# The last inverse step in operands of 128 rows, the last convolution ahead of the last attention rows, and a new order

## The chip, the core and the metric

The kernel runs on one core of one Trainium2 chip. The core has five engines that run side by side and wait for each other by semaphores: PE (matrix products, with a loader of weights shown as PEld), DVE and ACT (elementwise work; ACT alone has exp, sin and ln), POOL, and SP, which here only issues DMAs. Results of PE land in PSUM and have to be evicted by DVE or ACT into SBUF. The metric is the device time of one execution in microseconds (us), the median of several runs. A profiled execution also gives a span, first instruction to last, and a trace.

## What is computed

`x = A_u` has 2048 times and 512 channels (bf16). Two mixers read the same `x`, and a gate joins them:

```python
x = A_u
g = _sigmoid((x * gate_w).sum(-1, keepdims=True))
a = _A_ref(x, ...)      # S4 convolution: K[d,l] = Re sum_n C B dt exp(dt A l); y = irfft(rfft(u) rfft(K)); y + u * Dskip
b = _B_ref(x, ...)      # linear attention, 32 heads of 16, feature map [softmax(xW), softmax(-xW)], then @ wo
return g * a + (1 - g) * b
```

In `_A_ref` each channel has its own kernel `K` of 2048 times, a sum over 128 complex poles; the convolution is causal and padded to 4096. In `_B_ref` keys and queries go through `w_phi` and two softmaxes of 16 features, `kv` and `z` are sums over all times, and `o = phi_q kv / (phi_q z + 1e-6)`.

## The kernel before, in words

The 512 channels are cut into 4 quarters `Q` of 128 and 16 units of 32. The 2048 times are 16 blocks `j` of 128 rows of the tile `xT[time, j, Q, channel]`, which at first holds `x` and at the end the output. 512 rows (4 values of `j`) make one block `b` of the queries.

- **Head** (`prepare`, `keys_and_spectrum`, `attention_keys`). Parameters are loaded, sine tables are made on ACT (`TB`, `TI`, `TJ` for the transforms, `Ctab`, `Dtab`, `Gtab` for the poles), `x` is transposed (`xps`, `xT`), the spectrum of `x` is computed (`psAu`, `XAu`, `psBu`, `XU`) and written to DRAM as `XUd` (`xuw`), and the keys run through `pk2`, `ek2`, `vp2`, `vb2`, `kn2`. `gps` and `zps` are the products of the gate.
- **Queries** (`block(b, late)` in `plan_queries`). Blocks 0 to 2 are computed in the middle of the convolution, and the part of their result that belongs to Q = 3 is put into `xT` (`bs3`); for Q < 3 it is added inside the inverse step (`pya`). Block 3, the last 512 rows, is "late": `pqL`, `eqL`, `zsL`, the normalisers through DRAM (`awL`, `arL`, `emL`), `opsL`, `oTL`, and then `bpsL` with all 512 columns at once, into which the already computed convolution of Q < 3 is added out of `g.Y`. `bsg` scales its columns 0 to 383 by the gate, `outL` stores them; columns 384 to 511 (`bs3`) go to `xT` for the inverse step of Q = 3.
- **Convolution** (`plan_conv`). For each unit `kgen` builds the kernel: `A1`, `A2` (L1053) and, where `FOURS` has a 0, `A3` (L1064) make a table `A`; `Rh` (L1071) and `Rl` (L1075) make `R`; `kps` (L176) multiplies them (128 products, or 64 where `A3` has summed), `KD` and `XA` are evictions, `psA` the first transform. `transform` then works on a group of units: `psB`, `XK`, the product with the spectrum of `x` (`t`, L1185), `psz` and its eviction `Zr`, a write to DRAM (`zw`, L1230), a read back in another layout (`zr`, L1239, into `ZT`), the last inverse step `psy` (L1295) with the table `TJ`, and `ou` (L1320), which scales by the gate into `xT`. Groups: two pairs of units each for Q = 0, 1, 2, then units 12 and 13 together (64 channels), 14 alone (32 channels), and 15 alone, which does not go through DRAM (`pszn`, `Zn`, `psyn`).
- **Last inverse step.** In `psy` the even and the odd half of the 32 slots of a block sit in partitions 0 to 63 and 64 to 127 of `ZT` (`th` = 0 or 1), so each product uses 64 rows and 32 columns of PE: 4 products per `j`.

**What sets the order.** All work is first listed as nodes with `P.add` (engine, dependencies, the buffers it takes and drops) and `P.dma`. `Plan.run` then emits the nodes in the order written in the string `ORDER` (two digits per node), with `SIDES` choosing ACT or DVE for a node that may run on either, `RINGS` choosing the PSUM pool and `FOURS` the form of `kps`. The strings were found by a planner outside the file. On the chip each engine runs its own instructions in that order and waits by semaphores; SP and ACT issue DMAs in their order too, so a DMA that waits holds up those behind it. There are 8 lanes for DMAs in flight (`ln`): a DMA also waits for the one that used its lane before. When ACT changes between `T` (sine) and `L` (exp, ln), it loads another table (L65).

Of the kernel before, what the change touches and what calls it, by code (L numbers as in the profile page):

```python
# [43 lines left out]
def build_index_cols(nc, pool):  # L44
# [4 lines left out]
    f = pool.tile([128, len(want)], F32, name="if")  # L49
# [6 lines left out]
    return t, f, {name: f[:, k:k + 1] for k, (name, _, _) in enumerate(want)}  # L56
# [14 lines left out]
class Plan:  # L71

    DIGITS = "0123456789abcdefghijklmnopqrstuvwxyzABCDEFGHIJKLMNOPQRSTUVWXYZ-_"
    ORDER = ("0J0K0f0g0h0L0O0N0R0S2x0c0d0e0i0j0k1c1e0M1b000102030405090a0b1I1x0u0v0w0Y1d1o1z0U1f0x0y0z0V0P0W1A0607081p1B1q1J1K1Y0l0m0n"
             "0-0Z180_0X112P1g1-2y2N1Z2Q2B130r0s0t0A0B0C1_2A2O2C1y1C0o0p0q10190D0E0F2J2K2R1h1F1D0Q1G16122L2M2T2S2F142H2U2G171S2I2D2E2V"
             "2X2W152Y4v4w1N1O1r1s1t1i1j1k4u4B4C1E4J2v2w0G0H0I1H4F4K4D4N1Q0T1a2Z4E2-2_1U1V1P301W4G4x4O1M1l1m1n4L4M591X27314H1u1v1w4R4I"
             "28214P32335a1T344V4S3520224Q2324361L4T4U55374W4X4Z56254Y393a384-51574_521R58263b3d4y3c503e535h2z2a3f5d545i293g5l3h5b2b5e"
             "3J3i5c2d5f5g5t3j5j3k5k5m2e3l3m3n3K3o3p5u5n5o5v3L5w2f3M2c2g3q3v3r5p5x3w2o2h5q3x2i3y3C3z3A3B5r5y3E3D3s3t3u3N3P3F3Q3G3H3I3O"
             "2q3R3S2k3T2j3V3X3Y3U3W3Z3-2l3_5s402m412p4342442r2s4546472n484a4f2t494h2u4b4g4m4o4i704c4d4e4p727r4n7t5z7q7s4j4k4l4q4r4s5A"
             "5B5C5D5E4t5I6_5F5G5H714z734A7674777968696a6b7c5J78757d7a7i7e7D7j6c7b7f5K7g7E7h9a6d6e7F7J9c6f5L7R7S7T7k6g7l7u6h6z7v7K7x7w"  # L80
             "7A7m5M5N7n8O6i6j6k7-7_806A5O7y7z8X6B7B8P7o8Y5P7p7C6l6m6n6p6q6r6o6C7G7H7I8K7U7V7W6t5Q8M6u8L8Q7L8U5R8V8N6s5S5T5U5V8ZaD8R6D"
             "5W5X5Y7MaE916E6F927N7P7O7Q6G5-5_606H9d8S6v9e9m9n5Z8T9f61818W6I828-8_996w62836x6J6K6L6M6N6O9ba-90639j6Pb06y93946Q6R6S6465"
             "896T8h9k8a8i6U6V8485669o6W8b9s9g678c9h7X7Y7Z6XaA8daC9t6Y6Z6-9i8p8qazaB9l9D9E9Fa_9597b18j969p9q8r988kaFaM9raJ8687889u8l8s"
             "8e8f8gaGaN9vaKcw9w9y8m8n8o8t9xbb9zcyaHaIcxaLbcb2aOaSaTb3czaPb49MaQb89N8D9A9B9C9Ocob9aRaUbhcs9UaV9Vbd8u8v8w8x8y8zb58A8B8C"
             "9P9Q8E9G9H9I8F9R9S9T9Wb6cAcBcCa0a1djdk8G8H9J9K9La2bsbtbub7cDa8a9cEcF8I9XcGcHcIaWba9Y8Jbie8a3aaaXe9dsaba4bvbwbxbedl9Z9-9_"
             "bfdpaYdqdtaZbgacbjcpcJcKcLcNcOcPbkcMblbncQadaeafdmamctdybodncqbmbBbCbJbKa5a6a7dobRbpbqbrbDdrcubEbSduagahaid7d8d9bFbLbMdz"
             "bZbNbybzbAanb-dvdwdxcrbTcvdAdBbUb_bGbHbIc0eaaobObPbQajakaldCbVeeefc1dEbWbXbYapdFdDdGebecaqc2c3c4ardOdHdPasdadbdceddIegeB"
             "eCeEeFdQdJdgdhdicbeDeheHeic5c6c7eGeIejdKcccddRcRekdSdddedfeJeKc8c9cacedLdMdNeLeMeNeOcfelemencScgcTdTdUdVchePeQeoawaxayeR"
             "cUeSatauaveTepdWdXdYcVcWdZd-d_cZcXcYclcmcneUeVc-e0eWeqeresc_d0cicjcke1d1d2d3eXeYeteuevewexeyeZe5e6e7e2e3e4e-e_d4d5d6ezeA"
             "f3f4f5f0f1f2")  # L90
    SIDES = ("101001110101011000000100111001111100000011000100010000111101010000000100001100000000010000000000000000000000100000000001"
             "00010111111100000001100101000000010")
    RINGS = ("001011011111010000001010010001001010010010100100100100000110001100010101011110011011000000000000000000001110000000000001"
             "01011110001100000000010111010011100111001011001010010100111100000111110")
    FOURS = ("0111111101111110")
# [96 lines left out]
def prepare(P, nc, g, evict, psum):  # L192
# [38 lines left out]
    S("ifc", lambda: nc.scalar.copy(out=F.fi[:], in_=F.ii[:]), r="ic0", w="ic1")  # L231
# [5 lines left out]
    def cols(e):  # L237
# [8 lines left out]
        e.tensor_scalar(out=o[:, 6:7], in0=b6, scalar1=-2.0 / 2048.0, scalar2=1.0 / 2048.0, op0=ALU.mult, op1=ALU.add)  # L246
        e.tensor_scalar(out=o[:, 8:12], in0=g.c128[:, 0:4], scalar1=g.icol["s5"], scalar2=None, op0=ALU.is_equal)
# [17 lines left out]
    def sine(out, v, kv, w, turn=False):  # L265
        S("tgs", lambda: act(out=out(), in_=(low(v()) if not turn else low(v()).rearrange("p (h t) -> p t h", h=2)), func=ACT.Sin, scale=TURN), r=kv, w=w, tab="T")
# [266 lines left out]
def keys_and_spectrum(P, nc, g, psum):  # L533
# [9 lines left out]
    for h in range(2):  # L543
# [30 lines left out]
        for r0 in range(0, 32, 4):  # L574
# [22 lines left out]
            def wr(h=h, r0=r0, box=box):  # L597
                for n, a in ((128, 0), (64, 128)):
                    nc.sync.dma_start(out=g.XUd[:, h, a:a + n, r0 - 4:r0 + 4, :].rearrange("d x r c -> x d (r c)"), in_=box.s[0:n].rearrange("p d r c -> p d (r c)"))
                box.s = None  # L600
# [30 lines left out]
def attention_keys(P, nc, g, psum, r):  # L631
# [19 lines left out]
    a = P.add("PE", "gps", ga, xt, take=[("ps", "b2")], rw=("wsm", ""))  # L651
# [125 lines left out]
def plan_queries(P, nc, g, psum, r):  # L777
# [14 lines left out]
    def block(b, late, yn=()):  # L792
# [110 lines left out]
        def out_mm(ps, i, j):  # L903
            for m in range(4):
                nc.tensor.matmul(ps, lhsT=g.oT[3][i // 2][:, m, 128 * (i % 2):128 * (i % 2) + 128], rhs=g.wo[:, m, :], start=(m == 0), stop=False,  # L905
                                 skip_group_check=True)
            nc.tensor.matmul(ps[:, 384:512], lhsT=xT[:, j, 3, :], rhs=at.diagD[:, 3, :], start=False, stop=True, skip_group_check=True)
            nc.tensor.matmul(ps[:, 0:384], lhsT=g.ident[:], rhs=g.Y[:, i].rearrange("p q d -> p (q d)"), start=False, stop=True, skip_group_check=True)
# [16 lines left out]
        for ip in range(2 if late else 0):  # L925
# [8 lines left out]
            def b3(j=j, box=box):  # L934
                return xT[:, j:j + 2, 3, :], box.ps[:, :, 384:512]

            def bg(k, j=j, box=box):
                o, i = xT[:, j + k, 0:3, :].rearrange("p k d -> p (k d)"), box.ps[:, k, 0:384]
# [12 lines left out]
        if late:  # L951
            def st(h):
                for c in (2 * h, 2 * h + 1):
                    (nc.scalar if P.cur.at == "ACT" else nc.sync).dma_start(out=g.out2d[:, 0:384].rearrange("(q j c) d -> c q j d", q=32, j=16, c=4)[c][:, 4 * b:4 * b + 4],
                                      in_=xT[32 * c:32 * c + 32, 4 * b:4 * b + 4, 0:3, :].rearrange("p j a d -> p j (a d)"))
# [64 lines left out]
def plan_conv(P, nc, g, psum, r):  # L1020
# [6 lines left out]
    T, on, yn, late = {}, [], [], []  # L1027

# [11 lines left out]
    def kgen(units, XA, new, split=False):  # L1040
# [58 lines left out]
        for cc in range(nu):  # L1099
# [24 lines left out]
            s = P.add("PE", "psA", sa, d + ([s] if cc else []) + ([XA.first] if XA.off else []), take=[psq] + (["XA0"] if new and cc == 0 and XA.off == 0 else []), drop=(["KD"] if cc == nu - 1 else []))  # L1124
# [5 lines left out]
    def load(Q, p):  # L1130
# [3 lines left out]
        def dma():  # L1134
            L.X = g.fpool.tile([128, 2, 1024], BF16, name="XUX", tag="XUX", bufs=g.P.k["XUX"])
            for i in range(2):
                if Q < 3:
                    nc.sync.dma_start(out=L.X[:, i].rearrange("p (h z) -> p h z", h=2), in_=g.XUd[Q, :, 64 * i:64 * i + 128, 8 * p:8 * p + 8, :].rearrange("h x r c -> x h (r c)"))
                else:
# [5 lines left out]
    def transform(XA, ready, Q, off, nd, far, Ls, last, co=0, free=True, split=False):  # L1145
# [122 lines left out]
        for j0 in range(0, 16, nj):  # L1268
# [75 lines left out]
            if two:  # L1344
                yn.append(P.add(("ACT", "DVE"), "Y", lambda oy=oy: P.copy(*oy()), [ya[0], y, o], drop=["psum"]))
# [227 lines left out]
```

## Time and profile before

| what | value |
|---|---|
| median of 3 runs | 270.79 us (268.94 to 270.85) |
| the profiled execution | 270.31 us, span 268.5 us |
| DVE busy | 224.2 us (83%), 300 instructions |
| ACT busy | 219.1 us (82%), 265 instructions, 23.1 us of them 18 table loads |
| PE busy | 202.2 us (75%), 4640 products; weight loads 140.5 us (52%) |
| DMA | 36.27 MB, mean 135 GB/s |

How to read it: the rows of groups give line, engine, operation, result <- operands with partitions x elements, the count, then busy us and mean ns of one, then idle time of the engine just before and what ended it. Rows of the timeline give start, length, engine, line, operation, and idle time before with its releaser in brackets. An x2 merges two neighbours. A row of the waits gives who waited for whom, the total in us, how often, the longest. "SPq" and "ACTq" are DMA issues; their length is the time of the issue, not of the transfer.

### The profile page before, as it was taken

How to read it: one execution, taken by the hardware profiler on the slowest of the kernel's cores; microseconds unless marked ns; L12 is line 12 of the kernel's file. 1: busy time of each engine (PE TensorE's matmuls, PEld its weight loads, DVE VectorE, ACT ScalarE, POOL GpSimd, SP SyncE). 2: the span in 40 equal slices, each digit the busy share in tenths (PEclk: the TensorE clock that was granted, in tenths of full speed). 3: DMA queues.
4: the chain of work that ended last, by engine and by line, in shares of the span. 5: the costliest groups of instructions: out<-in, count | busy, mean ns of one | idle time of the engine just before them, and what ended most of it. 6: DMA issues, size and time to landing. Idle time of an engine off the chain costs nothing. (4 is left out here: it accounts for less than half of the span.)

```text
span 268.5 us, 10262 instructions
## 1 busy us (share of the span) xinstructions
PE 202.2 (75%) x4640; PEld 140.5 (52%) x4640; DVE 224.2 (83%) x300; ACT 219.1 (82%) x265; POOL 7.6 (3%) x16
## 2 busy tenths in 40 slices
PE   1358999999886679758587877876978779789810
PEld 1247666566655434435466755464747547665600
DVE  6999768698999789999999989995999889976401
ACT  6899799989899899999999989996788897644100
POOL 7300000000000000000000000000000000000000
PEclk9999999999999959999569999996897999999955
DMA  5999510000439894048055441392686899998372
GB/s 116 145 179 224 143 42 2 1 2 2 120 95 257 243 277 160 5 115 213 6 166 147 105 156 35 128 173 68 196 258 188 168 219 246 201 235 151 60 110 44
DMA packets 71468, 36.27 MB, mean 135 GB/s; under 512 B 50304, under 2 KB 66304, under 8 KB 71424
## 3 DMA queue, kind: packets, MB, share of 16 engines
q1 hardware_dynamic: 67680, 34.83, 56.0%
q10 hardware_dynamic: 3744, 0.79, 1.6%
q8 instruction: 36, 0.59, 0.9%
q14 instruction: 8, 0.07, 0.1%
HBM read 21.12 MB, written 13.11 MB: 127 GB/s over the span
## 5 line engine op out<-in xcount | busy, mean ns | idle before, releaser
L1053 DVE TENSOR_TENSOR A<-Ctab,Dtab 128x2048 bf16<-128x2048 bf16 x32 | 38.3, 1221 | 0.2
L68 ACT ACTIVATE cs<-args 128x1024 bf16<-128x1024 f32 x32 | 30.9, 1037 | 1.9 <-issue 1.1
L65 ACT ACT_TABLE_LOAD x18 | 23.1, 1283 | 0.3
L176 PE MATMUL kps<-R,A 128*32 128x64 bf16 x1856 | 20.3, 202 | 3.3 <-issue 2.1
L176 PEld LDWEIGHTS <-A 128*32 128x32 bf16 x1856 | 18.3, 116 | 6.6 <-issue 5.3
L1071 DVE TENSOR_TENSOR R<-E,cs 128x2048 bf16<-128x2048 bf16 x16 | 19.5, 1220 | 0.6 <-ACT E L68 0.6
L140 ACT CAST XK<-psB 128x1024 bf16<-128x1024 f32 (+1 forms) x15 | 14.3, 980 | 6.5 <-PE psB L189 6.3
L1075 DVE TENSOR_TENSOR R<-El,cs 128x2048 bf16<-128x2048 bf16 x16 | 19.5, 1220 | 0.1
L1185 DVE TENSOR_TENSOR t<-XUX,XK 128x2048 bf16<-128x2048 bf16 x14 | 17.1, 1220 | 2.1 <-ACT XK L140 1.3
L1217 PE MATMUL psz<-t,TI 128*128 128x512 bf16 x60 | 16.1, 395 | 2.8 <-ACT cs L68 2.6
L806 PE MATMUL pq<-xT,Wqp 128*128 128x512 bf16 x64 | 15.8, 393 | 2.6 <-ACT KD L140 2.2
L140 ACT CAST Zr<-psz 128x1024 bf16<-128x1024 f32 x15 | 15.3, 1032 | 2.7 <-PE psz L1217 1.2
L140 ACT CAST XA<-psA 128x1024 bf16<-128x1024 f32 (+1 forms) x15 | 13.9, 972 | 3.9 <-PE psA L183 3.8
L189 PE MATMUL psB<-XA,TB 128*128 128x128 bf16 (+2 forms) x192 | 11.2, 207 | 7.3 <-issue 3.3
L68 ACT ACTIVATE Ek<-pk 128x1024 bf16<-128x1024 f32 x16 | 15.4, 1024 | 1.4 <-PE pk L679 1.3
L68 ACT ACTIVATE E<-args 128x1024 bf16<-128x1024 f32 x16 | 16.4, 1042 | 0.2 <-PE args L1004 0.2
L68 ACT ACTIVATE Eq<-pq 128x1024 bf16<-128x1024 f32 x16 | 15.5, 1061 | 0.6 <-PE pq L806 0.6
L1320 DVE TENSOR_TENSOR xT<-psy,gT 128x1024 bf16<-128x1024 f32 (+1 forms) x5 | 5.6, 1116 | 11.8 <-PE psy L1295 11.8
L710 PE MATMUL vp<-WW,xT 128*128 128x512 bf16 x64 | 15.0, 379 | 0.0
L679 PE MATMUL pk<-WW,xT 128*128 128x512 bf16 x64 | 15.0, 379 | 0.0
L189 PEld LDWEIGHTS <-TB 128*128 128x128 bf16 x192 | 9.4, 100 | 9.7 <-issue 9.2
L497 PE MATMUL xps<-ident,UD 128*128 128x128 bf16 x64 | 7.3, 293 | 7.6 <-DMA UD<-in_A_u_dram 5.6
(203 smaller groups left out, 488.6 us busy)
## 6 DMA issues: line engine op xcount, KB each, us to landing
XUX<-XUd SPq DMA_DIRECT2D x32, 256.0 KB, 4.3
XUd<-xst SPq DMA_DIRECT2D x8, 512.0 KB, 4.4
ax<-apd SPq DMA_DIRECT2D x16, 256.0 KB, 5.2
Zd<-Zr SPq DMA_DIRECT2D x15, 256.0 KB, 3.6
ZT<-Zd SPq DMA_DIRECT2D x6, 512.0 KB, 7.2
UD<-in_A_u_dram SPq DMA_DIRECT2D x16, 128.0 KB, 4.3
XUd<-xst SPq DMA_DIRECT2D x8, 256.0 KB, 5.4
out_dram<-xT SPq DMA_DIRECT2D x4, 192.0 KB, 4.2
```

What stands on the lines that cost most here:

```text
L65: return self.nc.scalar.preload_act_table_set(name)
L68: return self.nc.scalar.activation(**kw)
L140: self.nc.scalar.copy(out=o, in_=i)
L176: nc.tensor.matmul(kps[32 * dj:32 * dj + 32, g4, e, :], lhsT=A[:, d // 4, 32 * ka:32 * ka + 32, d % 4], rhs=R[:, kr, d, :], start=(i == 0) ...
L189: nc.tensor.matmul(ps[:, sl, :], lhsT=fc.TB[:, 3 * (r0 + sl) + 1:3 * (r0 + sl) + 3].rearrange("p a b -> p (a b)"), rhs=XA[:, r0 + sl], sta ...
L679: nc.tensor.matmul(box.ps[:, u, :], lhsT=xT[:, 2 * s2 + u, kt, :], rhs=g.WW[:, kt, :], start=(kt == 0), stop=(kt == 3))
L806: nc.tensor.matmul(box.ps[:, m - m0, :], lhsT=g.Wqp[:, kt, 128 * m:128 * m + 128], rhs=xT[:, 4 * b:4 * b + 4, kt, :], start=(kt == 0), sto ...
L1053: nc.vector.tensor_tensor(out=c.A[:, :, 64 * k:64 * k + 64, :].rearrange("p q (x b) l -> p x b q l", b=8), in0=cf.unsqueeze(2).to_broadcas ...
L1071: nc.vector.tensor_tensor(out=c.R[:, :, :, 32:64], in0=t.E[:].unsqueeze(1).to_broadcast([128, 2, 32, 32]), in1=t.cs[:], op=ALU.mult)
L1075: nc.vector.tensor_tensor(out=c.R[:, :, :, 0:32], in0=t.L[:].unsqueeze(1).to_broadcast([128, 2, 32, 32]), in1=t.cs[:, ::-1, :, ::-1], op=A ...
L1185: nc.vector.tensor_tensor(out=box.t, in0=Ls[r0 // ns].X[:], in1=box.XK[:].unsqueeze(1).to_broadcast([128, 2, 1024]), op=ALU.mult)
L1217: nc.tensor.matmul(box.ps[:, hb, :], lhsT=fc.TI[:, k].rearrange("p t h a -> p (t h a)"), rhs=box.t[:, k, 512 * hb:512 * hb + 512], start=( ...
```

## The change

1. **The last inverse step of the far groups** takes 128 rows: `ZT` now holds the (x, r) rows of one time pair in all 128 partitions, 16 slots per read, and `TJ` is masked once (`tjm`) so that odd slots keep only the upper, even slots only the lower 64 rows. Two products per `j` of 128 rows and 64 columns replace four of 64 x 32. Since unit 15 still needs the unmasked table, it is saved to DRAM first (`tjw`) and read back as `TJ2` into one of the 4 `cs` buffers (`tjr`). `TI` changes its inner order to suit.
2. **Units 12 to 14 go ahead of block 3.** For them `psy` takes blocks `j` < 12 from `xT` as before and for `j` = 12 to 15 only the skip term; the result for these four goes to `g.Y` (now 4 quarters), and `bpsL` adds it: 480 columns out of `g.Y`, 32 from the skip term. `bsg` scales 480 columns, `outL` stores 448, the last store (units 14 and 15) waits for `bsg` as well.
3. **Layouts.** `XUd` is laid out so that a load of Q < 3 is one DMA with runs of 2 KB. `ZT` of 64 channels takes an `XUX` buffer and of 32 channels a `Zr` buffer instead of the single `ax`.
4. **A new order**, new sides, rings and forms: `FOURS` sums the tables of units 0, 6, 12 and 14 instead of 0, 8 and 15.

```diff
-    FOURS = ("0111111101111110")
+    FOURS = ("0111110111110101")
...
-    a = P.add("PE", "gps", ga, xt, take=[("ps", "b2")], rw=("wsm", ""))
+    a = P.add("PE", "gps", ga, xt + [sp], take=[("ps", "b2")], rw=("wsm", ""))
...
-            nc.tensor.matmul(ps[:, 384:512], lhsT=xT[:, j, 3, :], rhs=at.diagD[:, 3, :], start=False, stop=True, skip_group_check=True)
-            nc.tensor.matmul(ps[:, 0:384], lhsT=g.ident[:], rhs=g.Y[:, i].rearrange("p q d -> p (q d)"), start=False, stop=True, skip_group_check=True)
+            nc.tensor.matmul(ps[:, 480:512], lhsT=xT[:, j, 3, :], rhs=at.diagD[:, 3, 96:128], start=False, stop=True, skip_group_check=True)
+            nc.tensor.matmul(ps[:, 0:480], lhsT=g.ident[:], rhs=g.Y[:, i].rearrange("p q d -> p (q d)")[:, 0:480], start=False, stop=True, skip_group_check=True)
...
+    def tjw():
+        g.TJd = g.dram.tile([128, 64, 32], BF16, name="TJd")
+        nc.sync.dma_start(out=g.TJd[:], in_=fc.TJ[:])
+
+    def tjm():
+        nc.vector.tensor_scalar(out=fc.TJ[:, 1::2, :], in0=fc.TJ[:, 1::2, :], scalar1=g.icol["b6"], scalar2=None, op0=ALU.mult)
+        nc.vector.tensor_scalar(out=fc.TJ[:, 0::2, :], in0=fc.TJ[:, 0::2, :], scalar1=g.icol["nb6"], scalar2=None, op0=ALU.mult)
...
+            if Q < 3:
+                d = g.XUd[Q, p]
+                nc.sync.dma_start(out=L.X[:], in_=bass.AP(d.tensor, d.offset, [[1024, 128], [64 * 1024, 2], [1, 1024]]))
+                return
...
+        zt = {128: "ax", 64: "XUX", 32: "Zr"}[nd]
...
-            nc.sync.dma_start(out=F.Z[64 * th:64 * th + 64], in_=F.Zd[:, 2 * th:2 * th + 2].rearrange("t x r d -> (x r) t d"))
+            nc.sync.dma_start(out=F.Z[:, 16 * th:16 * th + 16], in_=F.Zd[16 * th:16 * th + 16].rearrange("t x r d -> (x r) t d"))
...
                     for jj in range(nj):
-                        th = (j0 + jj) // 8
-                        rows = slice(64 * th, 64 * th + 64)
-                        for c in range(4):
-                            nc.tensor.matmul(box.py[32 * c:32 * c + 32, jj // nr, jj % nr, :], lhsT=fc.TJ[rows, 4 * (j0 + jj) + c, :],
-                                             rhs=F.Z[rows, 4 * (j0 - 8 * th + jj) + c, :], start=False, stop=True, tile_position=(64 * th, 32 * c),
-                                             skip_group_check=True)
+                        for c in range(2):
+                            m = 2 * (j0 + jj) + c
+                            nc.tensor.matmul(box.py[64 * c:64 * c + 64, jj // nr, jj % nr, :], lhsT=fc.TJ[:, 2 * m:2 * m + 2, :].rearrange("p h q -> p (h q)"),
+                                             rhs=F.Z[:, m, :], start=False, stop=True, tile_position=(0, 64 * c), skip_group_check=True)
...
-    late += r["block"](3, True, yn)
+
+    def tjr():
+        g.TJ2 = g.csp.tile([128, 64, 32], BF16, name="TJ2", tag="cs", bufs=4)
+        nc.sync.dma_start(out=g.TJ2[:], in_=g.TJd[:])
+    g.tjr = P.dma("tjr", 0.45, 2.0, tjr, [g.tjw, sq], take=["cs"], move=1.8)
     L, first = [load(3, p) for p in range(4)], None
     for k, (units, far) in enumerate(g.LAST):
...
+        if XA.drop:
+            late += r["block"](3, True, yn)
         done = kgen(units, XA, True, units in g.SPLIT)
```

Where the order puts the nodes that the prediction speaks of: on PE the end is now `kps` of unit 15, `psA`, `psz` of unit 14, `psB32`, `pya`, `psy128`, `pya` (both halves of Q = 2), the first half of `pszn`, `psy64`, `opsL`, `psy128`, `psy32` (unit 14), the second half of `pszn`, `bpsL` twice, `psyn32` twice. Before it was `kps` of unit 15, the second half of Q = 2, `psA`, `psy128`, `opsL`, `psB32`, `psz` of unit 14, `bpsL` twice, `pszn`, `psy64`, `psyn32` twice, `psy32`. On SP the reads of unit 14 follow its write with one other read between, and the stores of the output come behind them. In the head the table loads of ACT in front of the first `E` go from 8 to 13 (one more, at L231, is the same in both), behind it from 10 to 7.

More of the change, by code (lines that the diff above doesn't have):

```diff
@@ L1344, in transform @@
             if two:
[L1345 removed]
+                yn.append(P.add(("ACT", "DVE"), "Y", lambda oy=oy: P.copy(*oy()), (ya or [y]) + [y, o], drop=["psum"]))
+            if end and Q == 3 and last:
+                on.extend(r["on"])
             if end and Q != 0 and (nd > 32 or last):
```

113 lines of the change are left out of this document (61 added, 52 removed).

## The prediction

> **What bounds the kernel now.** I read the table of stages first: busy time of each engine in four stretches that I cut at two instructions of VectorE (DVE): the first table product of unit 0 (L1053, at 99.71) and the end of the last right-hand product of unit 15 (L1075). Columns: stretch, its length, busy PE, PEld, DVE, ACT, POOL, then the granted clock of PE, DMA share and GB/s.
>
> ```profile
> span 268.5 us, 10262 instructions
> 0.00:99.70 99.70, 77.07 (x1043) 52.51 (x1044) 85.02 (x151) 90.19 (x116) 7.59 (x16) 0.97 0.55 122
> 99.70:235.20 135.50, 106.62 (x2967) 74.74 (x2966) 126.19 (x131) 122.24 (x140) 0.00 (x0) 0.92 0.59 148
> 235.20:255.00 19.80, 16.99 (x559) 12.36 (x558) 11.83 (x17) 6.66 (x11) 0.00 (x0) 0.99 0.74 149
> 255.00:268.50 13.50, 1.56 (x74) 0.93 (x73) 1.12 (x2) 0.00 (x0) 0.00 (x0) 0.50 0.54 78
> ...
> 233.94 1.22 DVE L1075 TENSOR_TENSOR R<-El,cs 128x2048 bf16<-128x2048 bf16 x1
> ```
>
> Three regimes. In the head DVE is idle for 99.7 - 85.0 = 14.7 us and ACT for 9.5, both waiting on each other and on PE. In the middle DVE is the bound: 126.2 of 135.5, idle 9.3. From 235.2, where the last right-hand product ends (233.94 + 1.22; call that moment T), nothing is dense: 33.3 us in which DVE works 13. So the head and the middle are priced by work moved onto or off DVE and ACT, and the tail by its chain of waits. For that I read the instructions in order of time.
>
> ```profile
> 244.72 1.03 ACT L140 CAST Zr<-psz 128x1024 bf16<-128x1024 f32 x1
> 245.88 0.43 SPq L1230 DMA_DIRECT2D Zd<-Zr  x1
> 253.19 0.84 SPq L1334 DMA_DIRECT2D out_dram<-xT  x2
> 257.00 2.56 SPq L1239 DMA_DIRECT2D ZT<-Zd  x2
> 263.05 0.40 PE L1295 MATMUL psy<-ZT,TJ 64*32 64x32 bf16 x32 [1.64 <-DMA ZT<-Zd]
> 263.55 0.69 DVE L1320 TENSOR_TENSOR xT<-psy,gT 128x512 bf16<-128x512 f32 x1 [6.36 <-PE psy L1295]
> 264.27 1.27 ACTq L1334 DMA_DIRECT2D out_dram<-xT  x2
> ...
> SPq L1334 <- DMA out_dram<-xT: 7.1, 2, 6.9
> SPq L1239 <- DMA out_dram<-xT: 2.8, 1, 2.8
> ```
>
> Unit 14's last block is evicted at 244.72 and written at 245.88, but its read back (L1239) is issued only at 257.00: SP stands in front of output stores and of that read until earlier stores have landed (the last two rows, from the waits of the DMA queues). The read's second half reaches PE at 263.05, DVE scales at 263.55, the store follows. The end hangs on when that read is issued. Earlier in the tail PE ran block 3 of the attention (bps).
>
> **The change, part by part.**
>
> *The head (to 99.7).* The new order changes sides. By count of the nodes in front of unit 0's first product, DVE takes on two more XU evictions, two more vb2, one xT copy, selE and diagD (from POOL) and two maskings of TJ, and gives up one wpe. ACT gets the mirror image and five more table loads (13 for 8).
>
> ```profile
> L142 DVE CAST xst<-psB 128x1024 bf16<-128x1024 f32 x8 | 9.6, 1221 | 1.8 <-DMA XUd<-xst 1.4 <-PE psB L587 0.3
> L140 ACT CAST xst<-psB 128x1024 bf16<-128x1024 f32 x8 | 7.8, 1047 | 0.0
> DVE  6999768698999789999999989995999889976401
> L375 DVE TENSOR_TENSOR Dtab<-Dtab,trg 128x1024 bf16<-128x1024 bf16 x8 | 5.3, 686 | 0.1
> L413 DVE TENSOR_SCALAR Ctab<-Ctab 128x1024 bf16<-128x1024 bf16 x2 | 0.8, 423 | 0.0
> L65 ACT ACT_TABLE_LOAD x18 | 23.1, 1283 | 0.3
> 27.36 1.76 PE L641 MATMUL gps<-gw,xT 128*128 128x1 bf16 x64
> ```
>
> DVE: 4 - 1 = 3 casts of this size at 1.22 = 3.7; selE, diagD and xT at no more than the 0.69 of a bf16 1024 row = 2.1; two maskings at 0.42 = 0.8: +6.6. ACT: 5 x 1.28 = 6.4, less four casts at 1.05, the wpe and the xT cancelling: +2.2. The gate's product gps (1.76 on PE) no longer stands in front of the first key product, so the key stage starts up to 1.8 earlier, and its time comes back later in a stage in which PE waits anyway. If DVE's 14.7 and ACT's 9.5 us of idle time cover everything, the head gains 1.8; if DVE's additions all lie on the path, it loses 6.6. I take +1: ACT, the fuller engine, gets 2.2 more, less 1.8, rounded up, since DVE, in the row of busy tenths (40 slices of 6.7 us), reads 9 8 9 9 9 in the slices 9 to 13 and has little room late in the head.
>
> The rule against it: the Trainium skill, "ScalarE: Activation LUTs", section "What ACT_TABLE_LOAD costs", puts a switch of set at about 2.66 us, 1.28 for the load and 1.38 for a drain. The trace does not show the second half:
>
> ```profile
> 71.92 1.28 ACT L65 ACT_TABLE_LOAD   x1
> 73.22 2.01 ACT L68 ACTIVATE trg<-pb 128x1024 bf16<-128x1024 int16 x2
> ```
>
> The next activation starts 1.30 after the load. By the page the five loads would cost 13.3 and ACT would be 9.1 heavier, its whole idle time; the row decides, and the sum stays.
>
> TJ is also copied to DRAM before it is masked, one more DMA of 512 KB on SP among the stores of the spectrum, and read back later as TJ2. SP's own issue time is small there, but behind the copy stands the read of statE and behind that the next spectrum store; the spectrum's buffers number three. Priced at 0, bounds 0 and the 1.4 us that DVE waited for such a store (the xst row). The loads of the spectrum shrink from two DMAs to one of twice the run length; DVE waits 0.7 in all for them (the row below), so 0 to -0.7, taken 0.
>
> *The middle (99.7 to T).* Per node: DVE loses one KD, one XA and one XK cast, gains another KD cast, loses unit 15's sum of tables (L1064) and gains those of units 6, 12 and 14 for that of 8, so one more of 1.22 net; one scaling (ou of Q = 1) moves behind T.
>
> ```profile
> L1064 DVE TENSOR_TENSOR A<-A 128x2048 bf16<-128x2048 bf16 x3 | 3.7, 1221 | 0.0
> DVE t L1185 <- DMA XUX<-XUd: 0.7, 1, 0.7
> 187.08 1.23 DVE L1320 TENSOR_TENSOR xT<-psy,gT 128x1024 bf16<-128x1024 f32 x1 [2.84 <-PE psy L1295]
> ```
>
> (1 + 1 - 1 - 1 - 1 - 1) x 1.22 = -2.4 on the bound engine. ACT gets two casts more and four loads less up to there, and has 13.3 us of idle time. The price of the new order itself, the stalls that it brings or takes, no row shows. Below: the one large stall (2.84, ending at 187.08 with an inverse step) goes. Above: as many stalls again as now, +9.3. I take none either way.
>
> The inverse step proper: 32 products of a 64*32 tile become 16 of a 128*64 tile with half the weights zero. That shape stands in the trace as psA:
>
> ```profile
> 239.98 0.63 PE L1295 MATMUL psy<-ZT,TJ 64*32 64x128 bf16 x32
> 239.41 0.64 PE L183 MATMUL psA<-W,KD 128*64 128x128 bf16 x16
> ```
>
> 0.63 against 0.64: no time on PE, fewer instructions. That the read now fills 128 partitions instead of 64 twice may speed it; I take the old time.
>
> *The tail (from T).* Before: T to the end is 33.3. After, in the new order, the tables of unit 15 are unsummed (128 products), then KD, psA, unit 14's psz and its eviction and write follow at once, and SP stands in front of nothing but reads:
>
> ```profile
> 228.73 0.39 PE L787 MATMUL psy<-wo 128*128 128x128 bf16 x4
> 231.87 0.64 PE L183 MATMUL psA<-W,KD 128*64 128x128 bf16 x16
> 226.21 1.39 PE L176 MATMUL kps<-R,A 128*32 128x64 bf16 x128
> 238.60 0.37 ACT L140 CAST KD<-kps 128x256 bf16<-128x256 f32 x1 [2.64 <-DVE KD L142]
> 243.57 1.02 PE L1217 MATMUL psz<-t,TI 128*128 128x512 bf16 x4
> Zd<-Zr SPq DMA_DIRECT2D x15, 256.0 KB, 3.6
> 244.44 1.03 PE L905 MATMUL bps<-wo,oT 128*128 128x512 bf16 x4
> 248.85 2.31 PE L1251 MATMUL psz<-TI,t 128*32 128x64 bf16 x128
> L942 DVE TENSOR_SCALAR xT<-bps,gT 128x384 bf16<-128x384 f32 x4 | 2.3, 612 | 1.5 <-ACT xT L140 1.5
> 253.11 0.64 PE L1308 MATMUL psy<-Z,TJ 64*32 64x16 bf16 x64
> 251.28 0.88 ACTq L954 DMA_DIRECT2D out_dram<-xT  x2
> ```
>
> 1. kps 1.4 + two KD 0.7 + psA 0.6 + psz 1.0 + eviction 1.0 = T + 4.7 (before: 245.75 - 235.2 = T + 10.5, since oT, XK and half of bps' operands came between).
> 2. Write 3.6, then the two reads as now, from 257.00 to 263.05 = 6.05, then psy 0.4: T + 14.8.
> 3. What PE has meanwhile: the 17.0 of the third stretch, less bps (248.85 - 244.44 = 4.4), half of pszn 1.2 and psyn 2 x 0.64 = 1.3, plus the first half of Q = 2, today done before T (pya from 228.73 to 231.87 = 3.1, psy 0.6), plus 0.7 for the longer kps: at most 14.5. PE comes to this psy about when the read has landed; neither waits long.
> 4. Behind psy on PE: the other half of pszn 1.2, bps 4.4: T + 20.4. Its wait for the copied result of unit 14 (Y, on ACT) lies beside pszn and the first products.
> 5. ACT: one copy 0.4, two scalings of 480 instead of 384 columns at 0.7: T + 22.2. Then six DMA issues, 0.88 + 0.88 + 1.27 = 3.0, and from the end of the last issue to the end of the span what it is now, 268.5 - 265.54 = 3.0: T + 28.2. The branch over psyn, DVE and SP ends before that: psyn 1.3, a scaling and SP's own two issues.
>
> The tail gains 33.3 - 28.2 = 5.1. The wait that is added stands on PE: psy of unit 14 is ahead of pszn, bps and psyn, and everything behind it moves one to one with the read.
>
> **Sum.** The profiled execution took 270.31 (span 268.5 + 1.8 around it): + 1 - 2.4 - 5.1 = -6.5, so 263.8. The median shown, 270.79, is 0.5 above the profiled one; I forecast **264.3**.
>
> **The rivals.**
>
> *The head pays in full* (0.13). DVE's +6.6 all on the path: 270.8 + 6.6 - 2.4 - 5.1 = 269.9, no change. For it: the 9 8 9 9 9 above. Against: 14.7 us of idle time, and ACT, not DVE, is the fuller engine.
>
> *New stalls in the middle* (0.12). The order was laid out anew for 966 old and 9 new nodes; as many stalls again as today's 9.3 give 264.3 + 9.3 = 273.6, at the border of slower. For it: TJ2 holds one of the four cs buffers to the end and its read stands on SP ahead of the last write of Q = 0. Against: the engine loads are the same.
>
> *The last read is late and PE goes slow* (0.13), the case on the other side. Place: psy of unit 14, now ahead of bps. If SP queues as it does now, from the write at 245.88 to psy's end at 263.45, 17.6 us pass instead of 10.1: psy ends at T + 22.3 instead of 14.8. It decides from T + 20 on, where the gain of the tail is gone. And PE would then have stood for over 7 us: in the last stretch, where it waited so, the granted clock is 0.50 against 0.99 before it. pszn and bps (5.6) at half the clock cost 5.6 more: 264.3 + 7.5 + 5.6 = 277.4. The Trainium skill, "TensorE: Matmul & The Clock Gate", section "HAM oscillation", has the same rule, half clock after an idle window of some 3.4 us; by that rule even a wait of that length would do, and the row agrees. Against it: in the new order of SP, unit 14's two reads have no store of the output in front of them.
>
> *Better than that* (0.07): the stall at 184 goes too and the head gains its 1.8: 264.3 - 2.8 - 2.8 = 258.7. *The 128-row step does nothing by itself*: that is in the forecast already, at 0.
>
> **How the numbers follow.** Forecast case 0.55, better 0.07, head 0.13, middle 0.12, late read 0.13. Within 1%, about what a measurement of this kernel tells from no change, is 268.1 to 273.5. Faster: 0.55 + 0.07 = 0.62. No change: the head and 0.05 of the middle, 0.18. Slower: the rest of the middle and the late read, 0.20. Range 258 to 275: it takes in better, head and middle and leaves out the late read and a little below, under 0.2.
>
> **What the profile will show.** Right: unit 0's first table product at 99 to 102; the end of the last R<-El product at 232 to 236; SP's read of unit 14 issued within 5 us of its write; psy of 32 columns about 15 us after T; some 13 us from there to the end, bps in it at a clock near 1. Wrong: a first table product after 105 (head), DVE idle for over 15 us in the middle, SP waiting for stores in front of L1255 or a clock of 0.5 under bps.

## The result

The changed kernel takes 262.46 us (median of four executions, 261.1 to 266.1) against 270.8: 0.9691 of the time before, with a 95% interval of 0.9625 to 0.9758. It is **faster by 3.1%**, 1.8 us below the forecast of 264.3. The changed kernel's first profile fell on its longest execution, so the rows here are from its repeat (`again`, profiled at 261.36 us); the only other profile below that is of a kernel's longest execution is that of `pd3` (263.96 us).

### The profile after

First the stretches of the repeat, cut at the same two instructions as before and then within the tail (columns as in the prediction: after the busy times come the granted clock of PE, the DMA share and GB/s):

```profile
0.00:101.90 101.90, 77.56 (x1033) 54.17 (x1043) 89.52 (x162) 92.75 (x117) 3.99 (x13) 0.92 0.55 125
101.90:228.67 126.77, 100.53 (x2731) 68.66 (x2737) 123.30 (x129) 119.70 (x139) 0.00 (x0) 0.96 0.57 164
228.67:235.60 6.93, 4.10 (x187) 3.29 (x189) 3.04 (x4) 3.74 (x6) 0.00 (x0) 1.00 0.67 120
235.60:239.00 3.40, 3.40 (x36) 3.33 (x33) 1.89 (x3) 0.01 (x1) 0.00 (x0) 0.51 0.85 169
239.00:259.60 20.60, 14.04 (x425) 10.32 (x424) 8.55 (x15) 3.19 (x6) 0.00 (x0) 0.91 0.70 115
```

Head 101.9 (was 99.7), middle 126.8 (135.5), tail 259.6 - 228.67 = 30.9 (33.3). The gain stands in the middle, not in the tail where I had put most of it. In the middle VectorE's work fell by 126.19 - 123.30 = 2.9 and its idle time from 9.31 to 126.77 - 123.30 = 3.47, by 5.8.

The tail in order of time, same kernel:

```profile
227.44 1.23 DVE L1089 TENSOR_TENSOR R<-El,cs 128x2048 bf16<-128x2048 bf16 x1
...
233.42 0.61 PE L1233 MATMUL psz<-t,TI 128*128 128x512 bf16 x2 [1.88 <-DVE XA L144]
234.10 1.01 ACT L142 CAST Zr<-psz 128x1024 bf16<-128x1024 f32 x1 [2.26 <-PE psz L1233]
235.14 0.33 SPq L1246 DMA_DIRECT2D Zd<-Zr  x1
...
235.52 3.38 SPq L1255 DMA_DIRECT2D ZT<-Zd  x3
...
245.34 0.68 PE L1312 MATMUL psy<-ZT,TJ 128*64 128x32 bf16 x32
...
251.76 1.22 ACT L943 ACTIVATE xT<-bps,gT 128x480 bf16<-128x480 f32 x2
...
254.90 1.46 ACTq L1354 DMA_DIRECT2D out_dram<-xT  x2
```

The read of unit 14 (two of the three reads at 235.52) now stands right behind its write, with no store in between. Its psy at 245.34 waits for no DMA. The reads were issued by 237.8 and landed within 4.7 us, so by 242.5. What is late is PE itself: it stands still for 1.88 us inside unit 14's psz (the profile names VectorE's XA, which had ended 0.85 us earlier; in `late_read`, below, the same stall is 2.10 with no releaser), and from 235.6 to 239 it runs at a granted clock of 0.51.

### The profile page after: what moved, and what is told of

It reads as the page before. It is cut to its first block, busy times and chain, and to the rows that moved or that the text cites. A ratio compares the mean times of both kernels' runs of the same rounds, so it can differ in the third digit from the quotient of the medians.

```text
span 264.3 us, 9822 instructions
## 1 busy us (share of the span) xinstructions
PE 198.2 (75%) x4404; PEld 139.6 (53%) x4424; DVE 226.5 (86%) x311; ACT 220.0 (83%) x267; POOL 4.0 (2%) x13
## 5 line engine op out<-in xcount | busy, mean ns | idle before, releaser
L142 ACT CAST XK<-psB 128x1024 bf16<-128x1024 f32 (+1 forms) x16 | 15.9, 1027 | 2.3 <-PE psB L191 1.8
L142 ACT CAST XA<-psA 128x1024 bf16<-128x1024 f32 (+1 forms) x15 | 14.8, 1029 | 0.5 <-PE psA L185 0.5
L809 PE MATMUL pq<-xT,Wqp 128*128 128x512 bf16 x64 | 14.9, 379 | 0.2 <-ACT Eq L70 0.2
L185 PE MATMUL psA<-W,KD 128*64 128x128 bf16 x256 | 10.1, 227 | 5.9 <-ACT KD L142 2.2
L144 DVE CAST xst<-psB 128x1024 bf16<-128x1024 f32 x10 | 11.8, 1217 | 3.1 <-DMA XUd<-xst 2.3
L590 PE MATMUL psB<-XAu,TB 64*128 64x128 bf16 x256 | 10.5, 233 | 4.4 <-DVE xst L144 2.9
L185 PEld LDWEIGHTS <-KD 128*64 128x64 bf16 x256 | 8.4, 113 | 9.5 <-issue 5.3
## 6 DMA issues: line engine op xcount, KB each, us to landing
UD<-in_A_u_dram SPq DMA_DIRECT2D x16, 128.0 KB, 4.2
```

The lines of the kernel that those rows point to most:

```text
L142: self.nc.scalar.copy(out=o, in_=i)
L185: nc.tensor.matmul(ps[64 * ri:64 * ri + 64], lhsT=lhsT, rhs=fc.W1[:, ri].rearrange("p r d -> p (r d)"), start=True, stop=True, tile_positi ...
L809: nc.tensor.matmul(box.ps[:, m - m0, :], lhsT=g.Wqp[:, kt, 128 * m:128 * m + 128], rhs=xT[:, 4 * b:4 * b + 4, kt, :], start=(kt == 0), sto ...
```

## The experiments

Times and ratios of all kernels, and their stages in the profiled execution (first table product of unit 0; T, the end of the last right-hand product; span). The kernel before took 270.2 to 272.1 (medians) beside them, so the ratio compares better than the time. Against it, with a margin of 2%, `again`, `rows64`, `after_shift` and `pd3` are faster, and `late_read` and `before_shift` the same. For `before_read`, `stat`, `tj_late`, `xu_old` and `best` the verdict is unclear, though their whole intervals lie below 1; `pool` ran once.

| kernel | us | ratio to before (95%) | first product | T | span | head / middle / tail |
|---|---|---|---|---|---|---|
| before | 270.8 | | 99.7 | 235.2 | 268.5 | 99.7 / 135.5 / 33.3 |
| again | 262.7 | 0.969 (0.961 to 0.977) | 101.9 | 228.7 | 259.6 | 101.9 / 126.8 / 30.9 |
| rows64 | 262.2 | 0.966 (0.956 to 0.976) | 101.8 | 231.1 | 260.5 | 101.8 / 129.3 / 29.4 |
| late_read | 269.2 | 0.993 (0.989 to 0.998) | 101.6 | 228.2 | 266.5 | 101.6 / 126.6 / 38.3 |
| before_read | 267.2 | 0.986 (0.976 to 0.996) | 99.7 | 235.3 | 263.6 | 99.7 / 135.6 / 28.3 |
| after_shift | 262.1 | 0.966 (0.960 to 0.971) | 102.6 | 231.3 | 260.2 | 102.6 / 128.7 / 28.9 |
| before_shift | 270.4 | 0.995 (0.987 to 1.003) | 100.8 | 234.0 | 267.8 | 100.8 / 133.3 / 33.8 |
| pd3 | 261.2 | 0.961 (0.953 to 0.969) | 101.6 | 230.8 | 262.2 | 101.6 / 129.2 / 31.4 |
| pool | 263.0 (one) | | 102.0 | 229.8 | 261.1 | 102.0 / 127.8 / 31.3 |
| stat | 260.0 | 0.969 (0.958 to 0.980) | 99.1 | 226.1 | 256.5 | 99.1 / 126.9 / 30.4 |
| tj_late | 259.8 | 0.965 (0.955 to 0.975) | 99.2 | 225.8 | 255.6 | 99.2 / 126.7 / 29.8 |
| xu_old | 260.9 | 0.971 (0.963 to 0.979) | 101.0 | 227.9 | 259.7 | 101.0 / 126.9 / 31.8 |
| best | 260.0 | 0.961 (0.954 to 0.968) | 99.3 | 227.3 | 260.3 | 99.3 / 128.0 / 33.0 |

### The changed kernel again

> The changed kernel once more, for a profile of an execution at the median. Theory A (the gain stands mostly in the tail and the middle): 262.5 us, first table product of unit 0 at 101 to 102, end of the last right-hand product of unit 15 at 231.5 to 233, tail 28 to 29. Theory B (the tail gained nothing but what the first profile showed, 2 us, and the gain stands ahead of it): tail 31 and the last right-hand product at 229 to 230.

B, nearly: the tail at 30.9 is B's, and T came at 228.7, 0.3 ahead of its range. So three things had to be explained: a longer head, a middle 6 us better than worked out, and a tail 2.7 worse.

### Is it the 128-row step? (rows64)

```diff
-    for c in range(2): ... lhsT=fc.TJ[:, 2 * m:2 * m + 2, :], rhs=F.Z[:, m, :]
+    for c in range(4): ... lhsT=fc.TJ[rows, 4 * (j0 + jj) + c, :], rhs=F.Z[rows, 4 * (j0 - 8 * th + jj) + c, :]
-    F.Z[:, 16 * th:16 * th + 16] <- F.Zd[16 * th:16 * th + 16]
+    F.Z[64 * th:64 * th + 64] <- F.Zd[:, 2 * th:2 * th + 2]
```

> The changed kernel with the last inverse step of the far groups taken back to four products of 64 rows and 32 columns per block, the table TJ unmasked, and the two reads per group each filling 64 partitions; the order stays. Theory A (the step itself is worth nothing): within 1 us of the changed kernel, that is 261.5 to 263.5 us, psy at 0.63 per 32 products, DVE less by the two maskings. Theory B (the read into 128 partitions is what brings unit 14 early): the read takes 7 us instead of 5.5, PE's last inverse steps come 1.5 to 3 us later, 264 to 265.5 us.

The largest psy group (128 columns wide) by shape (busy us, mean ns of one record, idle before), for `rows64` and then for the changed kernel:

```profile
L1312 PE MATMUL psy<-ZT,TJ 64*32 64x128 bf16 x192 | 3.8, 217 | 0.0
```

```profile
L1312 PE MATMUL psy<-ZT,TJ 128*64 128x128 bf16 x96 | 3.8, 222 | 0.0
```

The reads on their pages (count, KB, us to landing), in the same order:

```profile
ZT<-Zd SPq DMA_DIRECT2D x6, 512.0 KB, 6.3
```

```profile
ZT<-Zd SPq DMA_DIRECT2D x6, 512.0 KB, 5.5
```

Theory A: 192 products take the same 3.8 us as 96 of twice the rows and columns, the read lands 0.8 later, and the time is the same, 0.966 against 0.969. The step named first in the change is worth nothing that can be measured in the time. By stages it is less clear: the middle of `rows64` is 2.5 us longer and its tail 1.5 shorter. Its program has 160 products more, which also moves the PE stalls treated below, so the stages can't be laid to the step alone.

### What the early read is worth (late_read, before_read)

```diff
 late_read, SP:    zw#14 zr#7
-  zr#8 zr#9 out#1 out#0 out#5
+  out#1 out#0 out#5 zr#8 zr#9
 before_read, SP:  zr#7 out#3 zw#14
-  out#2 zr#8 zr#9
+  zr#8 zr#9 out#2          (ZT of 32 channels in a Zr buffer)
```

Here zw#14 is unit 14's write, zr#8 and zr#9 its two reads, out the stores.

> The changed kernel with the two reads of unit 14 moved on SP behind three stores of the output. Theory A (everything behind the inverse step of unit 14 on PE moves one to one with the read, and PE goes slow while it waits): the read is issued 6 to 10 us later, the end comes 5 to 9 us later by the read alone, and up to 5.6 more with PE at half clock: 268 to 277 us. Theory B (the read is hidden behind PE's other work, which had up to 14.5 us): less than 2 us, 262 to 264.5 us.

> The kernel before with one thing of the change: the read-back of unit 14 goes into a buffer of the ring Zr instead of the single ax, and its two reads stand on SP right behind unit 14's write, ahead of the last store that waits. Theory A (the late read sets the end of the kernel before): the last inverse step ends at about 256 to 258 instead of 263.5, the end follows until the stores of block 3 are the last: 263 to 265.5 us. Theory B (the end is set by the stores and DMA traffic as a whole, the read is only the last of them): 268 to 271 us.

`late_read`, in order of time:

```profile
246.33 1.53 SPq L1255 DMA_DIRECT2D ZT<-Zd  x2
...
250.28 0.61 PE L1312 MATMUL psy<-ZT,TJ 128*64 128x32 bf16 x16 [5.52 <-DMA ZT<-Zd]
...
251.61 1.93 PE L1267 MATMUL psz<-TI,t 128*32 128x64 bf16 x64
```

and the stretch behind the wait (after the busy times, 0.50 is the clock):

```profile
250.00:253.50 3.50, 3.05 (x97) 2.71 (x97) 0.62 (x2) 0.27 (x1) 0.00 (x0) 0.50 0.36 62
```

PE waits 5.52 us for the read, its psy ends at T + 23.5 instead of T + 17.4, and the tail grows from 30.9 to 38.3, by 7.4: 6.2 up to the end of this psy, one to one. The other 1.2 come behind it, where the clock stays at 0.50 for 4.3 us, from the end of the wait to 254.6. That is theory A at its lower end, 269.2 us.

The trace of `before_read`:

```profile
248.99 2.46 SPq L1240 DMA_DIRECT2D ZT<-Zd  x2
...
256.49 0.22 PE L1309 MATMUL psy<-Z,TJ 64*32 64x16 bf16 x8 [2.28 <-issue]
...
257.18 0.69 PE L1296 MATMUL psy<-ZT,TJ 64*32 64x32 bf16 x64
```

The read is issued 8 us earlier than in the kernel before, the last psy ends at 257.9 instead of 263.5, 5.6 earlier, and the tail falls by 5.0 to 28.3. The psy no longer waits for a DMA: a stall of PE of 2.28 us right in front of it is what holds it now. The ratio, 0.986, says 3.9 us (1.4% of 270.8), with 1.2 to 6.6 us in its interval. So moving one pair of reads in the old kernel, and giving them a buffer of another ring, already gives in its profile the tail that I had forecast for the whole change.

### Why PE stands still where nothing holds it (before_shift, after_shift)

In the kernel before, VectorE's one long wait (2.84 us, ending at 187.08) was for a psy behind a stall of PE. These are the stalls of PE over 1 us, with the releaser "issue" (no wait that the profile shows), in order of time:

```profile
183.55 0.80 PE L189 MATMUL psB<-XA,TB 128*128 128x128 bf16 x6 [3.28 <-issue]
...
200.97 0.89 PE L176 MATMUL kps<-R,A 128*32 128x64 bf16 x84 [1.35 <-issue]
...
242.22 0.72 PE L891 MATMUL ops<-Eq,KVbd 128*128 128x256 bf16 x5 [1.18 <-issue]
...
256.48 0.22 PE L1308 MATMUL psy<-Z,TJ 64*32 64x16 bf16 x8 [2.01 <-issue]
```

and this is the row of the page on the DMA queue that carries instructions (packets, MB, share):

```profile
q8 instruction: 36, 0.59, 0.9%
```

Each breaks a group of products in the middle: 6 left of 8, 84 of 128, 5 of 8, 8 of 64. Counted in PE's program (each product has a weight load; a few semaphore instructions come in addition), these places are instructions 5569, 6337, 8385 and 9153, which all leave 193 when divided by 256. Counted in the same way, the stall of 1.88 us in the changed kernel, for which the profile names VectorE, stands at 7873, which leaves 193 too. And 36 packets in 0.59 MB are 16 KB each; the kernel's 2 x 4640 loads and products are 36 times 256 and a rest. To test it I put products in front of PE's first one, whose result is overwritten:

```diff
             box.ps = psum([128, 2, 512], "psri")
+            for q in range(108 if not hasattr(g, "pad") else 0):      # 112 in before_shift
+                nc.tensor.matmul(box.ps[c:c + 32, 0, 0:64], lhsT=g.ident[:, 0:32], rhs=g.ident[:, 0:64], ...)
+            g.pad = True
```

> The kernel before with 112 idle products of 32 columns in front of PE's first product; nothing else. Theory A (the stall of 3.3 us under psB at 180, from which VectorE's one long wait of 2.84 us comes, goes with the place in PE's program, and a large part of the middle's gain is that the new order lost it): the stall and VectorE's wait at 184 to 187 are gone, the middle is 2 to 3 us shorter, the time 267.5 to 269.5. Theory B (the new order itself packs VectorE, and places in PE's program don't matter): the stall stays at psB, 270.8 or up to 1 more.

> The changed kernel with 108 idle products of 32 columns put in front of PE's first product, where PE waits for loads; nothing else. Theory A (the stall of 1.9 to 2.1 us that PE has in front of the second product of unit 14's psz, releaser 'issue', comes with the place in PE's program: such stalls stand a multiple of 256 PE instructions apart): the stall leaves psz, Zr of unit 14 is written about 2 us earlier counted from the last right-hand product, a shorter stall of about 1 us stands at psB behind it, and the time falls by 1 to 2 us, to 260.5 to 261.7. Theory B (the stall comes from a wait that the profile doesn't show, at that product): it stays at psz and the time is that of the changed kernel, 262.5, or up to 1 more for the products.

`before_shift`:

```profile
186.68 0.57 PE L1299 MATMUL psy<-ZT,TJ 64*32 64x128 bf16 x26 [1.43 <-issue]
...
187.29 1.23 DVE L1324 TENSOR_TENSOR xT<-psy,gT 128x1024 bf16<-128x1024 f32 x1 [1.17 <-PE psy L1299]
...
232.00 0.34 PE L791 MATMUL psy<-wo,oT 128*128 128x128 bf16 x3 [2.49 <-issue]
```

The stall under psB is gone, a shorter one stands inside the psy behind it, VectorE's wait falls from 2.84 to 1.17, and the middle from 135.5 to 133.3. But a stall of 2.49 appears at the end of the middle, 2 us ahead of T, the head is 1.0 longer and the tail 0.5, so the time is the same within its interval: theory A for the mechanism, B for the time.

`after_shift`:

```profile
189.69 0.23 PE L178 MATMUL kps<-R,A 128*32 128x64 bf16 x4 [1.31 <-issue]
...
233.73 1.04 PE L1237 MATMUL psz<-t,TI 128*128 128x512 bf16 x3
...
234.84 1.01 ACT L142 CAST Zr<-psz 128x1024 bf16<-128x1024 f32 x1 [0.42 <-PE psz L1237]
...
236.59 0.52 PE L191 MATMUL psB<-XA,TB 128*128 128x32 bf16 x14 [0.79 <-issue]
...
245.50 0.68 PE L1316 MATMUL psy<-ZT,TJ 128*64 128x32 bf16 x32
```

Unit 14's psz runs through, the rest of the stall stands at psB behind it, PE keeps its clock, and psy ends at 246.18, which is T + 14.9. The tail is 28.9, 2.0 less. A middle that is 1.9 longer, with a new stall of 1.31 in it, and a head that is 0.7 longer give it back: 0.966 against 0.969, no difference. Every stall of PE over 0.5 us with this releaser after the first 100 us, in these kernels and in `before_read`, `rows64` and the changed one, stands at a multiple of 256 plus 193. That the place in the program decides is shown; that PE waits there for the next 16 KB of its program is the reading that fits, and no row names it.

The Trainium skill, "Runtime: NRT & Kernel Launch", section "Instruction fetch mechanics", says that programs are refilled in blocks of 16 KiB, or 256 instructions. The trace agrees: 36 packets of 16 KB and stalls a multiple of 256 instructions apart. The same section of the Trainium skill calls the crossing of a boundary mostly hidden; here PE stood for up to 3.55 us at one place (`before_read`, psB at 184.8).

### What the head hangs on (pd3, pool, stat, tj_late)

```diff
 pd3, ACT:      tgs p_d#3 tgs ... p_sn p_sn tgs p_g   ->   p_d#3 moved in front of p_g (18 table loads for 20)
 pool:          selE and diagD on POOL instead of VectorE
 stat, SP:      statE reads moved from behind the copy of TJ to the front of the first spectrum store
 tj_late:       copy of TJ on SP behind the spectrum stores and two loads; maskings in front of a table product of unit 4
```

> The changed kernel with one exponential of the head (the node p_d#3) moved behind the sines, so that ACT loads its table two times less (18 for 20); nothing else. Theory A (ACT is what the head hangs on, and its 2.55 us more of busy time are the 2.2 us that the head got longer): the first table product of unit 0 comes 2 to 2.6 us earlier, at 99.3 to 99.9, and the time falls by as much, to 260 to 260.6. Theory B (VectorE's 4.5 us more of busy time are): the first product stays at 101.5 to 102, the time at 262.5.

> The changed kernel with selE and diagD made on POOL again instead of VectorE. Theory A (ACT is what the head hangs on): the first table product of unit 0 stays within 0.5 us of 101.9, though VectorE has 2 to 3 us less to do. Theory B (VectorE): it comes 1.5 to 2.6 us earlier.

The first table product in `pd3`:

```profile
101.61 2.36 DVE L1067 TENSOR_TENSOR A<-Ctab,Dtab 128x2048 bf16<-128x2048 bf16 x2
```

and in `pool`:

```profile
102.01 2.36 DVE L1066 TENSOR_TENSOR A<-Ctab,Dtab 128x2048 bf16<-128x2048 bf16 x2
```

Against 101.90, taking 2.6 us off ACT moves it by 0.3, and taking two operations off VectorE by nothing. By these profiles neither engine sets the head, so both of my theories fell. The times don't say so as clearly: `pd3` has a ratio of 0.961, 2.2 us below the changed kernel by it, with overlapping intervals, and its head stands in one profile only. The DMA issues of SP were next. In the kernel before:

```profile
68.39 28.35 SPq L599 DMA_DIRECT2D XUd<-xst  x16
```

In the changed kernel, again:

```profile
73.11 1.14 SPq L602 DMA_DIRECT2D XUd<-xst  x2
74.34 0.71 SPq L1035 DMA_DIRECT2D TJd<-TJ  x1
75.10 5.79 SPq L354 DMA_DIRECT2D statE<-pz  x8
80.99 17.87 SPq L602 DMA_DIRECT2D XUd<-xst  x14
```

The spectrum's 16 stores ended at 96.74; now two stand ahead of the copy and of 5.8 us of small reads, and the last is issued at 98.86, 2.1 later, just what the head lost. The trace of the changed kernel shows how this reaches the engines. Both wait for a buffer xst until a store of the spectrum has landed:

```profile
91.95 1.01 ACT L142 CAST xst<-psB 128x1024 bf16<-128x1024 f32 x1 [0.66 <-DMA XUd<-xst]
91.97 1.22 DVE L144 CAST xst<-psB 128x1024 bf16<-128x1024 f32 x1 [0.81 <-DMA XUd<-xst]
```

and PE, whose results they evict, works to the end of the head at half the clock, where in `stat` (below) it keeps the full one. These are the stretches of the changed kernel and then of `stat`:

```profile
92.30:101.90 9.60, 7.42 (x118) 4.53 (x118) 8.59 (x20) 7.79 (x9) 0.00 (x0) 0.50 0.99 275
```

```profile
92.30:99.10 6.80, 4.10 (x102) 2.45 (x101) 6.37 (x16) 6.78 (x8) 0.00 (x0) 1.00 1.01 297
```

> The changed kernel with the eight reads of statE put back on SP ahead of the first spectrum store, as they stand in the kernel before; nothing else. Theory A (the head is 2.2 us longer because these reads, and the copy of TJ, stand between the first spectrum store and the others, so that SP issues the last of them at 98.86 instead of 96.74): SP starts the second spectrum store about 5 us earlier, the last one is issued at 97 to 98, the first table product of unit 0 comes 1 to 2 us earlier, at 100 to 101, the time 260.5 to 261.5. Theory B (the end of the head is set by the engines): first product at 101.5 to 102, 262.5 us.

> The changed kernel with the copy of TJ to DRAM moved on SP behind the spectrum stores and two loads, and the two maskings of TJ moved on VectorE from the head to the middle (in front of a table product of unit 4); nothing else. Theory A (the copy of 512 KB lengthens the head by what it takes of a DMA that is full in the spectrum's stores, 1.9 us at 270 GB/s): first table product 1.5 to 2.5 us earlier than 101.9, the middle 0.8 longer by the maskings, time 261 to 262. Theory B (the copy and the maskings cost nothing where they stand): first product within 0.9 of 101.9, and the time 262.5 to 263.5.

`stat`:

```profile
75.75 21.04 SPq L602 DMA_DIRECT2D XUd<-xst  x14
...
99.11 2.36 DVE L1067 TENSOR_TENSOR A<-Ctab,Dtab 128x2048 bf16<-128x2048 bf16 x2
```

`tj_late`:

```profile
79.78 17.16 SPq L602 DMA_DIRECT2D XUd<-xst  x14
...
99.17 2.36 DVE L1067 TENSOR_TENSOR A<-Ctab,Dtab 128x2048 bf16<-128x2048 bf16 x2
```

Either edit alone issues the last store at 96.8 or 96.9 and brings the first product 2.7 to 2.8 us earlier, more than either theory A had asked for. So it takes both the reads and the copy to cost this: with the reads moved ahead (`stat`) both waits above are gone, with the copy moved behind (`tj_late`) one of 0.48 is left, and PE keeps its clock in both. How much of the 2.7 is waiting and how much the half clock isn't separated. The ratios are too wide to resolve it. Against `xu_old`, run with them on the same chip, the two are 1.0 and 1.1 us lower.

### Is it the layout of the spectrum? (xu_old)

```diff
-    g.XUd = dram.tile([4, 4, 192, 2, 512], BF16, name="XUd")     # one load of 512 KB
+    g.XUd = dram.tile([4, 2, 192, 32, 64], BF16, name="XUd")     # two loads of 256 KB
```

> The changed kernel with the spectrum laid out in DRAM as before, each load of it two DMAs of 256 KB with shorter runs; nothing else. Theory A (the layout is worth nothing by itself, VectorE waited 0.7 us in all for these loads before): VectorE's waits for the spectrum in the middle stay under 1.5 us, time 262 to 263. Theory B (the fuller packing of VectorE in the middle rests on the faster loads): 2 to 4 us of such waits come back, 264.5 to 266.5.

The longest of VectorE's waits in the middle of `xu_old` (total, times, longest):

```profile
DVE Eq L876 <- DMA ax<-apd: 1.0, 2, 0.5
DVE t L1200 <- ACT XK L142: 0.9, 2, 0.5
```

VectorE waits for no spectrum, and the middle is 126.9. Theory A: the layout is worth nothing by itself in the middle. In the head the old layout even comes out 0.9 us shorter (101.0), with the last spectrum store issued at 97.85 instead of 98.86; one profile doesn't settle that.

### Together (best)

The edits of `stat`, `tj_late` and `pd3` in one kernel.

> The changed kernel with the three edits of the head together: the reads of statE ahead of the first spectrum store, the copy of TJ behind the stores and its maskings in the middle, and p_d#3 behind the sines (two table loads of ACT less). Theory A (each takes something of the same wait in the head, so that they add up only in part): first table product of unit 0 at 98 to 99, the rest as in the changed kernel, 0.950 to 0.960 of the kernel before, 257.5 to 260 us. Theory B (they undo each other or the later stages give it back): 0.965 to 0.970 of the kernel before, as the changed kernel.

The first product comes at 99.3, no earlier than with one edit alone: they remove the same wait. In the profiled execution (262.0 us, 2 above the median) the later stages give the gain back: the middle is 1.2 longer and the tail 2.1, with the stall in unit 14's psz at 2.05 and the half clock behind it over 6.8 us, twice as long as in the changed kernel. That is theory B for the profile. The ratio is 0.961 (0.954 to 0.968) against 0.969 (0.961 to 0.977) for the changed kernel: about 2 us lower, with intervals that overlap, and the same as that of `pd3` alone. Its interval lies below 1, but whether it beats the changed kernel isn't settled.

## Why the prediction was right or wrong

**Head: +1 forecast, +2.2 measured, and for the wrong reason.** I took it from ACT's table loads (+2.2) less the earlier keys. `pd3` gave ACT 2.6 us back and the head of its profile kept its length but for 0.3. The term that failed is the one that I priced at 0: the copy of TJ and the read of statE in front of the next spectrum store, with 1.4 as its upper bound. It measured 2.7 to 2.8, twice my bound. I had taken the bound from a wait of VectorE alone. In the changed kernel ACT and VectorE both wait for the spectrum's stores (0.66 and 0.81), PE is held up behind them and runs at a clock of 0.50 for the last 9.6 us of the head (the last 5.5 in the kernel before), which I had not counted at all.

**Middle: -2.4 forecast, -8.7 measured.** The work on VectorE was right: -2.9 in the table of stages for -2.4. The failed step is the price of the new order, which I took as "none either way": idle time fell by 5.8. A wait of 2.84 went with a stall of PE that depends on where a 256-instruction boundary falls; `before_shift` took 1.7 of it by padding alone. The other 3 us are short waits of 0.3 to 1.3. They aren't from the layout (`xu_old`), and they go with the kernels that have the new order: VectorE's idle time in the middle is 2.6 to 5.8 in all ten of them, against 9.3 and 9.5 in the kernel before and `before_read`, and 6.9 in `before_shift`. What in the order does it is not shown. The 128-row step is not ruled out (the idle time of `rows64` is 5.6, with a wait of 1.4 for a load of the spectrum in it), and the change of `FOURS` was not tried by itself.

**Tail: -5.1 forecast, -2.4 measured.** Once its stall is moved, in `after_shift`, the tail comes out close to what I had worked out: psy of unit 14 at T + 14.9 for 14.8, the last scaling on ACT at T + 21.9 for 22.2, the end at T + 28.9 for 28.2. The first agreement is partly luck. My step 2 had write and read end at T + 14.4 and set the psy, but the reads had landed by T + 12.5 (issued by 238.7, landing within 5.1), and psy waited for no DMA; PE's other work, 14.5 in my step 3, was what set it. In the changed kernel itself, step 1 took T + 6.4 instead of 4.7, because PE stood 1.88 us inside psz. That stall and 3.4 us at half clock, neither of them in my sum, fell on PE's own path, and psy ended at T + 17.4. From there on, my steps 4 and 5 hold: 13.6 us to the end for 13.4.

**The sum.** The errors were +1.2, -6.3 and +2.7 and partly cancelled; a forecast within 2 us doesn't mean that its terms were right. Of the signs that I had named, the last right-hand product missed its range (228.7 for 232 to 236) and psy of unit 14 ended at T + 17.4 for about 15; the first product, the issue of the read, the 13 us behind psy and the clock near 1 under bps came as said.

**The rivals.** The late read is real and one to one, but I overpriced it: `late_read` costs 6.5 us (269.2 against the 262.7 of `again` beside it), not 13.1. psy ended at T + 23.5, close to the 22.3 worked out, but that is only 6.2 later in a tail that already had PE late, and the half clock lasted 4.3 us behind the wait and cost about 1.2, not 5.6. The Trainium skill, "TensorE: Matmul & The Clock Gate", section "HAM oscillation", puts the half clock behind idle windows of some 3.4 us. The row of 235.6 to 239.0 shows 0.51 after a stall of 1.88, so here shorter gaps were enough. The clocks of all fourteen traces say what goes with it instead: the granted clock changes only at steps of 3.41 us, 72 of its 82 drops to 0.5 follow a step in which PE was busy for less than 48%, and of the 779 steps after which it stayed at 1.0 only two had so little. *The 128-row step does nothing* held as far as the time tells. *The head pays in full* did not come: +2.2 is near the forecast case, though by another mechanism. *New stalls in the middle* was the wrong sign.

## What to carry to other kernels

Read DMA issue order as carefully as engine load: two reads standing behind stores were worth 5 us of tail, and eight small reads together with a copy of 512 KB in front of a store 2.7 us of head, while 2.6 us off a nearly full engine moved the head of one profile by 0.3. A PE stall with no releaser in a program of thousands of small products should be located in the program; if such stalls sit at multiples of one distance, padding moves them, and a stage can gain or lose 1 to 3 us by a reorder that has nothing to do with its idea. Check a forecast by its stages, since errors of opposite sign hide in the sum.

## What the runs showed of the hardware

- PE stalls of 0.5 to 3.55 us that stand a multiple of 256 PE instructions apart, at different products in each kernel. The queue "instruction" moved 36 packets of 16 KB in the kernel before and 34 in the changed one, which has 216 products fewer.
- A granted clock of 0.51 over 3.4 us followed a PE stall of only 1.88 us; without that stall (`after_shift`) the clock stayed at 1.00 there. In all fourteen traces the clock changes at steps of 3.41 us, and 72 of 82 drops follow a step with PE busy for less than 48%; in 65 of the 82 steps PE was never idle for 2 us on end.
- Eight reads of 32 KB took 5.8 us of SP's issue time (`again`, 75.10), and ACT and VectorE waited for the stores behind them.
- 192 products of 64 rows and 32 columns took as long as 96 of 128 rows and 64 columns, 3.8 us each.
